# First tokens' softmax weights transposed in pairs of heads, and a fourth attention unit with float32 v

## The chip, the cores and the metric

The kernel runs on one core of a Trainium2 chip. The metric is the device time of one execution in microseconds. Before the change three executions took 577.93, 580.09 and 583.28 us, so the time before is their median, 580.09 us. One further execution was taken with the hardware profiler; it lasted 578.71 us, of which 576.9 us lie between the first and the last instruction that the profile shows.

## What is computed

Attention over 4 batches, 8 heads, 576 tokens of 64 elements, blended with a memory read, then a feed-forward block over all 2304 tokens:

```python
scores = scale * np.matmul(q, k.transpose(0, 1, 3, 2))      # causal
a = np.exp(scores - scores.max(-1, keepdims=True))
a /= a.sum(-1, keepdims=True) + 1e-09
local = np.matmul(a, v)
q_p = phi(q)
mem_out = einsum(q_p, M_prev) / (einsum(q_p, z_prev) + 1e-06)
g = 1.0 / (1.0 + np.exp(-beta))
attn = g * mem_out + (1 - g) * local
r = np.maximum(attn @ w_in, 0.0)                            # w_in 512x2048
out = (r * r) @ w_out                                       # w_out 2048x512
```

## The kernel before

The tokens of a batch are cut into tiles: the first 64 tokens (tile 0) and four tiles of 128 (tiles 1 to 4). The first 64 tokens of all four batches are done together, at the start, by `first_tokens` (L244); the rest is done by `attention` (L354), called once per unit. A unit is one batch, one pair of heads and either the tiles 1 and 2 ("lo"), 3 and 4 ("hi") or all four. The list `order` (L820) begins with the four lo units of batch 0 (units 0 to 3, here u0 to u3), then its four hi units (u4 to u7), and so on. The feed-forward block works on 256 tokens at a time: `moe(0)` on the first tokens, `moe(1)` on tiles 1 and 2 of batch 0, and so on, and at the end `moe_pair` on two blocks together. `moe(0)` is interleaved with the units u1 to u3 while the weights are still being loaded and split into a rounded and a rest part (`split_weight`, L169: ScalarE, VectorE and GpSimd work on each piece). `moe(1)` needs the output of u0 to u3, which goes to DRAM (`xd`) and is read back (`xn`), apart from the last pair of heads, u3, whose tile `memx` is transposed straight from SBUF (`prefetch`, L625, argument `tail`).

Each engine executes its instructions in a fixed order. That order is made when the program is built, by a scheduler that estimates when each instruction can run; it is not written out by hand, so an edit in one place can move instructions in others.

`first_tokens` packs two batches into a group g (two groups), with eight slots i (batch and pair of heads), and in each slot head 0 in the partitions 0 to 63 and head 1 in the partitions 64 to 127. `scores` (L272) fills `sp0`, `softmax` (L297) makes the weights `e` from it on VectorE and ScalarE, `outputs` (L311) transposes them by sixteen 64x64 matmuls with the identity (L315) into `px`, copies that on ScalarE to `wx` (L316), and accumulates M*f (L320) and v*wx (L321) in `xp`; from there ScalarE and VectorE make `xh` and `xl` (L326, L327), the input of `moe(0)`.

In `attention`, three flags go by the unit's place i in `order` (L837): `early` (i < 12), `sfull` (i < NES = 6: scores in float32) and `full` (i < NEF = 3, lo units alone: the softmax weights meet v in float32). With `full`, each tile's weights `e` are transposed on TensorE (L535, 64- and 128-column blocks, into `px`, named pxa), copied by ScalarE to `aT` (L540, named aF in the rows), and multiplied with `vv` in float32 (L579, acc). Without `full`, v is scaled to a power of two and split into two float16 halves `vs` (L405 to L428: vx, vt, vy, vz, vs), the weights are split into two float16 halves `a` (L558 on ScalarE, L560 on VectorE), a DMA transposes them (L564, `aT`), and L585 to L590 multiply on TensorE in float16; `s3` (L592) adds two column halves. Both ways end in L600, which adds to `memx`. The PSUM tiles pxa, pm (the memory read, L445), vt and acc all take turns in the two buffers of tag "av", so each waits until the one two places before it has been read. `kd` (the keys) has one buffer (KB = 1): the next unit's keys are loaded when the last scores of this unit are done.

## Time and profile before

| what | before |
|---|---|
| median of 3 executions | 580.09 us |
| profiled execution | 578.71 us, span 576.9 us |
| TensorE matmul (PE) busy | 550.8 us (95%) |
| VectorE (DVE) busy | 414.0 us (72%) |
| ScalarE (ACT) busy | 349.6 us (61%) |
| GpSimd (POOL) busy | 63.7 us (11%) |
| DMA, share of 16 engines' time | 49.7% |

Busy time is an average over stretches with different limits. In the profile's 40 slices of 14.4 us VectorE and ScalarE are near full in the first six, and TensorE is near full from the third to the last. A wait that the profile reports for an engine is idle time and what ended it; a matmul's end is modelled, so the distance between starts tells TensorE's pace better than the durations do. A float32 matmul shows as two instructions, a float32 transpose as one.

### The profile page before, as it was taken

What the parts mean: (1) busy time and instruction counts of PE and PEld (TensorE: products, weight loads), DVE (VectorE), ACT (ScalarE), POOL (GpSimd) and SP (SyncE); (2) the same over time, 40 slices, a digit from 0 to 9 for tenths busy, and PEclk for the clock granted to TensorE, in tenths of its full rate; (3) what the DMA queues carried; (4) which work ended last, traced back from release to release, by engine and by line L of the source; (5) the groups of instructions that cost most, each with busy time, mean ns of one, the idle gap of its engine ahead of it and who ended that gap; (6) DMA issues with size and microseconds to landing.
All of it is one profiled execution on the core that took longest, in us unless ns stands there. A gap on an engine that the chain in (4) does not pass through costs nothing.

```text
span 576.9 us, 11597 instructions
## 1 busy us (share of the span) xinstructions
PE 550.8 (95%) x4259; PEld 478.6 (83%) x4259; DVE 414.0 (72%) x1323; ACT 349.6 (61%) x792; POOL 63.7 (11%) x45
## 2 busy tenths in 40 slices
PE   5489998898999999999999999999999999999997
PEld 5378886787888888898988988889889898888885
DVE  6989989897989888989695988969787523212121
ACT  4589976767868767877567675665756222212213
POOL 3749560012010000000000000000000000000000
PEclk9999999799999999999999999999999999999999
DMA  8857654875665466676456736675244610000001
GB/s 310 341 192 286 228 168 111 174 162 136 138 150 159 109 183 151 149 185 168 110 108 124 149 78 163 115 189 143 56 84 83 128 37 1 36 2 0 1 0 73
DMA packets 124856, 74.71 MB, mean 129 GB/s; under 512 B 97152, under 2 KB 110464, under 8 KB 124800
## 3 DMA queue, kind: packets, MB, share of 16 engines
q1 hardware_dynamic: 124800, 73.98, 49.7%
q8 instruction: 33, 0.54, 0.4%
q14 instruction: 23, 0.19, 0.1%
HBM read 41.59 MB, written 8.78 MB: 87 GB/s over the span
## 4 chain that ended last, share of the span: by engine, by line
PE 63%; DVE 12%; ACT 10%; DMA 9%; issue 3%; POOL 1%; SPq 1%; ACTq 0%; DVEq 0%; POOLq 0%
PE oacc L677 8%; PE up L747 6%; PE up L749 6%; PE up L748 6%; PE oacc L737 6%; PE oacc L739 6%; PE oacc L738 6%; PE sp L479 5%; DMA vv<-in_qv_dram 4%; ACT e L520 3%; PE up L692 3%; PE up L691 3%; PE up L693 3%; PE acc L590 2%; PE pm L445 2%
## 5 line engine op out<-in xcount | busy, mean ns | idle before, releaser
L747 PE MATMUL up<-xh,w 128*128 128x256 f32 x448 | 129.5, 289 | 0.0
L748 PE MATMUL up<-xl,w 128*128 128x256 f32 x448 | 128.9, 288 | 0.0
L749 PE MATMUL up<-xh,w 128*128 128x256 f32 x448 | 128.4, 287 | 0.0
L520 ACT ACTIVATE e<-e,mx 128x320 f32<-128x320 f32 (+3 forms) x128 | 77.6, 608 | 50.1 <-DVE memx L600 34.1
L737 PE MATMUL oacc<-w,gh 128*128 128x512 f32 x224 | 89.9, 402 | 0.0
L747 PEld LDWEIGHTS up<-xh,w 128*128 128x128 f32 x448 | 86.0, 192 | 2.9 <-issue 0.6
L738 PE MATMUL oacc<-w,gh 128*128 128x512 f32 x224 | 88.4, 395 | 0.0
L748 PEld LDWEIGHTS up<-xl,w 128*128 128x128 f32 x448 | 86.1, 192 | 2.2
L739 PE MATMUL oacc<-w,gl 128*128 128x512 f32 x224 | 86.4, 397 | 0.4 <-DVE gl L759 0.4
L749 PEld LDWEIGHTS up<-xh,w 128*128 128x128 f32 x448 | 86.1, 192 | 0.7
L560 DVE SCALAR_TENSOR_TENSOR a<-e,a 128x128 f16<-128x128 f32 x116 | 64.1, 566 | 31.1 <-ACT a L558 30.1
L558 ACT ACTIVATE a<-e 128x128 f16<-128x128 f32 x116 | 55.0, 524 | 10.9 <-DMA aT<-a 9.9
L753 ACT ACTIVATE r<-up 128x512 f32<-128x512 f32 x56 | 32.7, 584 | 43.2 <-PE up L749 29.0
L702 DVE CAST gh<-r 128x512 fp32r<-128x512 f32 x15 | 6.4, 427 | 62.4 <-ACT r L701 62.4
L739 PEld LDWEIGHTS oacc<-w,gl 128*128 128x128 f32 x224 | 41.5, 188 | 9.0 <-DVE gl L759 0.9
L738 PEld LDWEIGHTS oacc<-w,gh 128*128 128x128 f32 x224 | 42.3, 189 | 6.6
L500 DVE CUSTOM_DVE_ANT_0 e<-sp,mask 128x320 f32<-128x320 f32 (+3 forms) x128 | 47.0, 417 | 0.9 <-PE sp L479 0.7
L737 PEld LDWEIGHTS oacc<-w,gh 128*128 128x128 f32 x224 | 42.3, 189 | 6.4
L700 ACT ACTIVATE r<-up 128x512 f32<-128x512 f32 x16 | 9.6, 597 | 60.8 <-PE up L693 60.8
L759 DVE TENSOR_TENSOR gl<-r,gh 128x512 fp32r<-128x512 f32 x56 | 38.9, 695 | 2.6 <-ACT gh L756 1.8
L677 PE MATMUL oacc<-w,gh 128*128 128x512 f32 x120 | 36.8, 389 | 0.0
L590 PE MATMUL acc<-vs,aT 128*128 128x128 f16 x302 | 36.7, 220 | 0.0
(153 smaller groups left out, 1160.2 us busy)
## 6 DMA issues: line engine op xcount, KB each, us to landing
raw<-in_w_in_dram SPq DMA_DIRECT2D x11, 512.0 KB, 7.2
vv<-in_qv_dram SPq DMA_DIRECT2D x16, 320.0 KB, 3.3
raw<-in_w_out_dram SPq DMA_DIRECT2D x9, 512.0 KB, 6.6
kd<-in_kk_dram SPq DMA_DIRECT2D x16, 288.0 KB, 3.1
out_dram<-o SPq DMA_DIRECT2D x16, 256.0 KB, 2.1
xd<-memx SPq DMA_DIRECT2D x31, 128.0 KB, 1.9
xn<-xd SPq DMA_DIRECT2D x14, 256.0 KB, 2.9
qm<-in_qv_dram SPq DMA_DIRECT2D x8, 321.0 KB, 2.9
```

The source lines that it names most:

```text
L500: nc.vector.tensor_tensor_reduce(out=e[:, h, ka:kb], in0=sps[:, h, cs], in1=mask[:, 448 - q0 + ka : 448 - q0 + kb], scale=-0.125, scalar=3 ...
L520: ex = nc.scalar.activation(e[:n, h, :ke], e[:n, h, :ke], AF.Exp, bias=bs, scale=-1.0, accum_out=sm[:n, h : h + 1])
L558: nc.scalar.mul(av[:, :, o0 : o0 + w], x, SC)
L560: nc.vector.scalar_tensor_tensor(out=av[:, :, o0 + w : o0 + 2 * w], in0=x, scalar=SC, in1=av[:, :, o0 : o0 + w], op0=ALU.mult, op1=ALU.sub ...
L590: nc.tensor.matmul(o2, aT[:, h * nb + c, :n], vs[:, h, c], start=False, stop=c == i)
L677: mms.append(nc.tensor.matmul(acc[t], g[:, ts], w_out_op(f, part), start=s0, stop=s1))
L737: nc.tensor.matmul(acc[t], gh[:, u, ts], w_out_op(f, 0), start=f == 0, stop=False)
L738: nc.tensor.matmul(acc[t], gh[:, u, ts], w_out_op(f, 1), start=False, stop=False)
L739: nc.tensor.matmul(acc[t], gl[:, u, ts], w_out_op(f, 0), start=False, stop=f == NF - 1)
L747: nc.tensor.matmul(up[:, u, :], w_in_op(f, k, 0), xh[:, k, :], start=k == 0, stop=False)
L748: nc.tensor.matmul(up[:, u, :], w_in_op(f, k, 0), xl[:, k, :], start=False, stop=False)
L749: nc.tensor.matmul(up[:, u, :], w_in_op(f, k, 1), xh[:, k, :], start=False, stop=k == NK - 1)
```

## The change

It does two things, and what they need. First, in `first_tokens` the scores are laid out so that a pair of slots shares a column block: slot i's two heads stand side by side, in the partition half that i's parity chooses. `outputs` can then transpose two heads of two slots at once: four 128x128 transposes (L316 of the changed kernel) instead of sixteen 64x64 matmuls for each group. `softmax` starts with two operations on 128x4x64 instead of one on 128x512, `v` is multiplied with half-column slices of `ex`, and the gate g1b gets its own columns in the beta table (12 columns become 20). Second, NEF goes from 3 to 4, so that u3 takes the `full` way as u0 to u2 do.

```diff
-NEF = 3
+NEF = 4
...
         def scores(g):
-            sp[g] = sp0[:, g]
+            sp[g] = sp0[:, :, g]
             q, k = part(g, 0), part(g, GD)
-            for i, hd in pairs():
-                nc.tensor.matmul(sp[g][hd, i], q[hd, i], k[hd, i], start=True, stop=True)
+            for i in range(0, GN, 2):
+                for u, h in ((0, 0), (1, 1), (1, 0), (0, 1)):
+                    hd, ud = (slice(x * D, (x + 1) * D) for x in (h, u))
+                    nc.tensor.matmul(sp0[ud, h, g, i // 2], q[hd, i + u], k[hd, i + u], start=True, stop=True)
...
-            nc.vector.scalar_tensor_tensor(
-                out=e, in0=sp[g], scalar=0.125, in1=mask0[:, None, :].to_broadcast(bc), op0=ALU.mult, op1=ALU.add
-            )
+            bc = [P, GN, D]
+            for h in range(2):
+                nc.vector.scalar_tensor_tensor(
+                    out=e.rearrange("p (j h) k -> p j h k", h=2)[:, :, h], in0=sp[g][:, h], scalar=0.125,
+                    in1=mask0[:, None, :].to_broadcast([P, GN // 2, D]), op0=ALU.mult, op1=ALU.add,
+                )
...
         def outputs(g):
-            ex = tp.tile([P, GN, D], F32, tag="wx", name="wx", bufs=2)
-            px = ps.tile([P, GN, D], F32, tag="up", name="px0", bufs=2)
-            for i, hd in pairs():
-                nc.tensor.matmul(px[hd, i], et[g][hd, i], ident[hd, hd], start=True, stop=True)
+            ex = tp.tile([P, GN // 2, P], F32, tag="wx", name="wx", bufs=2)
+            px = ps.tile([P, GN // 2, P], F32, tag="up", name="px0", bufs=2)
+            for j in range(GN // 2):
+                nc.tensor.transpose(px[:, j], et[g][:, 2 * j : 2 * j + 2].rearrange("p h k -> p (h k)"), ident)
             gate["s"] = nc.scalar.copy(ex, px)
...
-                gate["t"] = nc.tensor.matmul(xp[hd, i], v[hd, i], ex[hd, i], start=False, stop=True)
+                qs = slice(i % 2 * D, (i % 2 + 1) * D)
+                gate["t"] = nc.tensor.matmul(xp[hd, i], v[hd, i], ex[hd, i // 2, qs], start=False, stop=True)
```

The scheduler orders the program anew. Three places matter here (line numbers of the changed kernel differ by up to 3 from those before).

On ScalarE, in the first tokens: the copies wx of the two groups stand between the casts of the weights w_102 to w_105. Before:

```order
L187 CAST w_104<-raw_511 128x512
L187 CAST w_103<-raw_496 128x512
L316 COPY wx<-px_279 128x512
L187 CAST w_105<-raw_518 128x512
L316 COPY wx<-px_343 128x512
```

And in the changed kernel:

```order
L184 CAST w_104<-raw_488 128x512
L317 COPY wx<-px_279 128x512
L184 CAST w_103<-raw_473 128x512
L317 COPY wx<-px_332 128x512
L184 CAST w_105<-raw_495 128x512
```

Both copies stand one place earlier. On VectorE, beside it, the second group's scaling of w now stands behind the weight operation that it stood in front of, so w_104's cast can start one operation earlier; and on TensorE the first matmul of the second group that waits for f no longer stands ahead of the first group's matmuls with wx.

On TensorE, where `moe(0)` has run its last matmuls whose weights are there, and u3's products with v stand (oacc is `moe(0)`, sp are u4's second scores). Before:

```order
L739 MATMUL oacc<-w_1240,gl 128x512
L445 MATMUL pm<-qm,pe 128x130 x2
L585 LDWEIGHTS aT
L585 MATMUL acc<-vs,aT 128x128
...
L479 MATMUL sp<-kd,qm 128x512 x2
L585 LDWEIGHTS aT
...
L414 MATMUL vt<-identb,vx 128x128
L635 MATMUL px<-identr,xn 128x128 x6
L637 MATMUL px<-identr,memx 128x128
L445 MATMUL pm<-qm,pe 128x130 x2
L479 MATMUL sp<-kd,qm 128x448 x2
L479 MATMUL sp<-kd,qm 128x64 x2
L747 MATMUL up<-xh,w_1091 128x256
```

And in the changed kernel:

```order
L741 MATMUL oacc<-w_1203,gl 128x512
L537 MATMUL pxa<-identr,e 64x128
L537 MATMUL pxa<-identr,e 128x128 x2
L537 MATMUL pxa<-identr,e 64x128
L537 MATMUL pxa<-identr,e 128x128 x2
L581 MATMUL acc<-vv,aF 128x64 x6
...
L637 MATMUL px<-identr,xn 128x128 x6
L639 MATMUL px<-identr,memx 128x128
L481 MATMUL sp<-kd,qm 128x512 x2
L581 MATMUL acc<-vv,aF 128x64 x4
L416 LDWEIGHTS vx
L416 MATMUL vt<-identb,vx 128x128
L749 MATMUL up<-xh,w_1054 128x256
```

u3's sixteen float16 products have become ten float32 transposes and ten float32 products; u4's pm and u5's first scores, which stood ahead of the next 24 up matmuls of `moe(0)`, stand behind them, and u3's pm stands eight oacc matmuls earlier.

On ScalarE, the copies aF of u3 (64- and 128-partition forms) and what stands between them, in the changed kernel; before, u3 had no such copies, and its L558 stood further ahead:

```order
L390 ACTIVATE pe<-qm 128x256
L542 COPY aF<-pxa 64x128 x2
L542 COPY aF<-pxa 128x256 x2
L522 ACTIVATE e,sm<-e,mx 128x448 x2
L560 ACTIVATE a<-e 128x2x64
L560 ACTIVATE a<-e 128x2x384
L542 COPY aF<-pxa 64x128 x2
L542 COPY aF<-pxa 128x128 x2
L642 CAST xh<-px 128x4x128
```

The copies of u3's second tile stand behind the exponentials and the scaling of u4's first tile (448 and 384 columns).

## Rows read from the trace of the kernel before

**Rows 1.** The page, its first part: busy time of the engines.
```profile
PE 550.8 (95%) x4259; PEld 478.6 (83%) x4259; DVE 414.0 (72%) x1323; ACT 349.6 (61%) x792; POOL 63.7 (11%) x45
```

**Rows 2.** Who TensorE waited for, 95 to 104.5 us: total, times, longest (us).
```profile
PE pm L445 <- DVE s L592: 1.2, 1, 1.2
PE acc L585 <- DVE vs L427: 1.1, 1, 1.1
PE sp L479 <- DMA kd<-in_kk_dram: 1.0, 1, 1.0
PE px L635 <- DMA xn<-xd: 0.3, 1, 0.3
```

**Rows 3.** Windows: length, busy PE, PEld, DVE, ACT, POOL; granted clock, DMA share, GB/s.
```profile
102.30:108.90 6.60, 5.58 (x24) 4.43 (x24) 5.71 (x23) 4.59 (x10) 0.84 (x1) 0.50 0.69 155
108.90:115.40 6.50, 6.46 (x67) 5.29 (x66) 5.25 (x17) 5.72 (x13) 0.00 (x0) 0.99 0.93 158
```

**Rows 4.** Timeline, first tokens: start, length (us), engine, line, [idle before <- by].
```profile
12.54 1.28 DVE L300 SCALAR_TENSOR_TENSOR w<-sp,mask 128x512 f32<-128x512 f32 x2
...
15.92 0.61 DVE L182 TENSOR_SCALAR raw<-raw 128x512 uint32<-128x512 uint32 x1 [0.32 <-DMA raw<-in_w_in_dram]
...
25.22 2.94 PE L315 MATMUL px<-identr,w 64*64 64x64 f32 x64 [0.35 <-DVE w L309]
...
26.41 0.66 ACT L187 CAST w<-raw 128x512 fp32r<-128x512 f32 x1 [1.87 <-DVE raw L184]
...
28.63 0.58 ACT L316 COPY wx<-px 128x512 f32<-128x512 f32 x1
...
29.26 0.27 PE L321 MATMUL xp<-wx,tr 64*64 64x64 f32 x1 [0.25 <-ACT wx L316]
```

**Rows 5.** Windows for line L315 alone: length, busy PE, PEld; granted clock, DMA share, GB/s.
```profile
25.20:26.20 1.00, 0.98 (x18) 0.98 (x20) 1.00 0.92 375
...
27.20:28.00 0.80, 0.80 (x32) 0.80 (x30) 1.00 0.05 20
```

**Rows 6.** Timeline of TensorE: what follows the last matmul of xp.
```profile
33.15 1.13 PE L479 MATMUL sp<-kd,qm 64*128 64x320 f32 x8
```

**Rows 7.** Timeline of TensorE, u3's float16 products and what follows each stretch.
```profile
96.97 0.22 PE L585 MATMUL acc<-vs,aT 128*128 128x128 f16 x1 [1.11 <-DVE vs L427]
...
97.72 1.13 PE L479 MATMUL sp<-kd,qm 64*128 64x512 f32 x4
98.78 0.23 PE L585 MATMUL acc<-vs,aT 128*128 128x128 f16 x1
...
99.07 0.22 PE L414 MATMUL vt<-identb,vx 128*128 128x128 bf16 x1
```

**Rows 8.** Timeline of TensorE, float32 products of u0 and what follows each stretch.
```profile
45.06 1.38 PE L579 MATMUL acc<-vv,aF 64*128 64x64 f32 x8
46.37 0.50 PE L739 MATMUL oacc<-w,gl 128*128 128x512 f32 x1
...
47.40 0.56 PE L579 MATMUL acc<-vv,aF 128*128 128x64 f32 x4
47.79 0.38 PE L535 MATMUL pxa<-identr,e 128*64 128x128 f32 x2
...
52.22 1.52 PE L579 MATMUL acc<-vv,aF 64*128 64x64 f32 x8
53.58 0.67 PE L445 MATMUL pm<-qm,pe 128*128 128x130 f32 x4
```

**Rows 9.** Timeline of TensorE and ScalarE: transposes and copies of u2; one scaling L558.
```profile
84.83 0.60 PE L535 MATMUL pxa<-identr,e 128*64 128x128 f32 x4
85.18 0.36 PE L747 MATMUL up<-xh,w 128*128 128x256 f32 x1
...
88.06 0.72 ACT L540 COPY aF<-pxa 64x128 f32<-64x128 f32 x4
...
98.14 1.04 ACT L558 ACTIVATE a<-e 128x128 f16<-128x128 f32 x2 [2.27 <-DMA aT<-a]
```

## The prediction

> **What bounds the kernel now.** I read the page's busy times first: TensorE's matmuls are busy 550.8 of 576.9 us, 95% [rows 1]. No other engine comes near, so the kernel ends when TensorE's work ends, and a change can move the time in three ways: it changes TensorE's work, its idle time, or the clock that it is granted. Next I read the table of waits over the stretch in which u3 meets v, since half of the change is there. It names 3.6 us in four waits (1.2 + 1.1 + 1.0 + 0.3) between 95 and 104.5 us [rows 2]. [...] Last I read the timeline of the first tokens, where TensorE waits for others. Its matmuls with the weights, L315, start at 25.22; ScalarE's copy wx(0) starts at 28.63 and takes 0.58; the first product with wx stands at 29.26 and waited for that copy [rows 4]; the last one ends at 33.15, where the scores of the next unit begin [rows 6].

> The profiled execution took 578.71 us. That is 1.4 below the median of the three runs (580.09); the sums below start from 578.71, and the range allows for that distance.

> **Part A, the first tokens.** Sixteen matmuls for a group become four transposes. Before, wx(0) stands behind the casts of w_104 and w_103 on ScalarE; the first of them starts at 26.41 and waited for VectorE [rows 4]. Now wx(0) stands behind w_104's cast alone, and on VectorE that cast's input stands one operation further ahead; a pass over 512 columns takes 0.61 there [rows 4], so the cast starts near 25.8, ends near 26.5 (0.66), and wx(0) ends near 27.0 instead of 29.21: 2.2 us earlier. wx(1) takes about the place that wx(0) had, ending at 29.2. The first product with wx no longer has the second group's wait for f ahead of it. From 29.26 to 33.15 [rows 4, 6] the 64 matmuls of both groups take 3.89, or 1.95 for a group. At the same pace the first group now runs 27.05 to 29.0, the second 29.2 to 31.15: **2.0 us earlier**. That is the best end.

> The worst end comes from the pace. Within L315 there are 18 matmuls in 1.0 us from 25.2, and 32 in 0.8 us from 27.2 [rows 5]: it doubles during L315, though the granted clock column reads 1.00 in both windows. I take that to be the rise of TensorE's clock to its higher level, after rb and 40 matmuls of L315. After the change only eight transposes stand where 64 matmul records stood (one for each transpose, two for each matmul), so there is less work ahead of xp, and the rise can fall into xp itself. If all of xp ran at the slow pace, it would take 7.8 us from 27.05, to 34.85: 1.7 later than before. If the rise comes at the end of the first group, that group ends at 30.95 and the second at 32.9: 0.25 earlier; if in its middle, 1.0 to 1.5 earlier. I take **-0.5** (bounds -2.0 and +1.7), since work like that of 25.2 to 27.0 had brought the rise before. What stands behind xp (ScalarE's and VectorE's xh and xl, the first up matmuls, and SP's load of the keys behind the scores) is released by it, and moves along.

> [...]

> VectorE gets two passes of 256 columns for each pass of 512 in the softmax (1.28 us for the two passes of before [rows 4]). Two halves cost at least the same and at most twice that, +0 to +1.3; I take +0.1, which the idle 0.32 us ahead of 15.92, ended by a DMA, hides [rows 4]. Without that cover it would move L315's start, and so A, by the same. The gate's beta table is one operation less; nothing.

> **Part B, u3 with v in float32.** TensorE's work:
> - taken away: the float16 products, 0.75 (96.97 to 97.72) and 0.29 (98.78 to 99.07) [rows 7], and vt, about 0.2: -1.24;
> - added: ten transposes; four take 0.35 in u2 (84.83 to 85.18) [rows 9], so 0.9;
> - added: ten products; in u0 tile 2's took 1.31 (45.06 to 46.37) and 0.39 (47.40 to 47.79), tile 1's 1.36 (52.22 to 53.58) [rows 8]: 3.06. Together +3.96 - 1.24 = **+2.7**.

> TensorE's waits: for vs, for s and for the keys' DMA [rows 2]. vs and s are steps of the float16 way and don't exist any more for u3. The keys' load is released by the last scores of the unit, which move up with them; xn comes from DRAM after u2, and is 0.3 us late only because nothing stands ahead of it. So **-3.6** at most, and the stretch is filled with 4 us of matmuls where it was thin. Does the clock then fall to 0.50? The fill brings me to say no: **-2.8** (bounds -2.8 and 0).

> New waits. The products follow their transposes at once, so TensorE waits for ScalarE's copies aF: for the first tile two of 64x128 (four took 0.72 in u2 [rows 9], so 0.36) and two of 128x256 (half of a 128x512 copy's 0.58 [rows 4] each): 0.9. For the second tile ScalarE first has u4's two exponentials and the scaling L558, 1.04 for two of 128 columns [rows 9], while TensorE has only six matmuls of px and the scores to do; I take 0.8 more. Together **+1.7** (bounds 0.9, the first tile alone, and 3.6, as much as TensorE waits there now). VectorE loses vx, vt, vs, L560 and L592 of u3, ScalarE exchanges L558 for the copies, two DMA transposes go: all beside TensorE.

> B: -3.6 - 2.8 + 2.7 + 1.7 = **-2.0**.

> **Part C, given back.** u4 uses float16 as before, and TensorE comes to it earlier than VectorE does; the wait for vs that u3 had (1.1 [rows 2]) can come back there: 0 to +1.1; I take **+0.5**.

> Sum: 578.71 - 0.5 - 2.0 + 0.5 = 576.7, say **576.7 us**, 0.6% below the median.

> **Rivals.**
> - R1, the clock stays low through all of xp, +1.7 in place of -0.5: 578.9. For it: only eight transposes are left ahead of xp [rows 5]. Against: rb's matmuls, too, stand before them, and xp's own matmuls bring a rise as L315's did. 14%.
> - R2, everything works: xp at full pace (-2.0), new waits only 0.9 (B -2.8), nothing given back: 573.9. For it: each of these steps has its row, and TensorE at 95% [rows 1] passes on whatever it saves. 25%.
> - R3, on the other side: ScalarE's queue holds u3's second copies back behind u4's exponentials, the stretch stays thin, TensorE waits 3.6 as before and the clock falls as before. Then B is the added work, +2.7, and the time 578.71 - 0.5 + 2.7 + 0.5 = 581.4. It decides from the point at which new waits exceed 3.7 with the clock kept, or 0.9 with the clock lost; of 1.7 expected, that is not far. 15%.
> - R4, the gain is given back later: VectorE and ScalarE are 72% and 61% busy as a mean [rows 1], and both are near full in the first 80 us. If u4 to u7 wait for them, TensorE arrives early and waits, B and C cancel: 578.2. 14%.

> **How the numbers follow.** My forecast has 32%, the four rivals 68%. Best case of all bounds: -2.0 (A), -3.7 (B with no new wait at all), 0 (C): 573.0. Worst: +1.7, +2.7, +1.1: 584.2. The range must leave out no more than 2 in 10: from 571.5 (the best case, and 1.4 of the distance between one execution and a median) to 582.5 (R3 with the whole of C). All but R3 lie below the profiled execution or within 0.2 of it. What a measurement of this kernel can tell from no change is about 1%: faster is below 574.3, slower above 585.9. Faster then holds most of R2 and a little of the forecast: 0.24. Slower lies 1.7 beyond even the worst sum; the distance between one execution and a median reaches most of that way: 0.08. Within 1%: 0.68.

> **What would show it.** wx(0)'s end (27.0 against 29.21) and the spacing of xp's matmuls show A: if the whole of xp takes 3.9 us, R1 is wrong; if the first scores behind it begin at 33.15 or later, A is. In the stretch 93 to 106, the table of waits must lose vs and s and show aF copies on ScalarE at 1.7; a granted clock near 1.00 where 0.50 stood shows B's clock term. If the clock still falls, I am 2.8 too low; if it falls somewhere else, in the units behind, too. For C, the wait of L585 for vs grows in u4. The forecast is wrong as a whole if the new order moves stalls to places that no part here names.

## The result, and the profile after

The changed kernel takes 587.27 us (median of 4 runs, 586.07 to 587.82) against 580.36 us before: ratio 1.0117, 95% interval 1.0086 to 1.0147. It is slower, by 1.2%; 576.7 had been forecast, and the range ended at 582.5.

The page of the changed kernel, first busy times and then the granted clock in 40 slices:

```profile
span 585.2 us, 11501 instructions
PE 556.0 (95%) x4216; PEld 483.0 (83%) x4216; DVE 408.3 (70%) x1310; ACT 350.7 (60%) x795; POOL 62.2 (11%) x45
...
PEclk9999998798999999999999999999999999999999
```

VectorE lost 5.7 us of work, as foreseen, and TensorE gained 5.2 [rows 1]. Windows around the float32 products of u3 and behind them (columns as in [rows 3]):

```profile
99.20:109.50 10.30, 9.80 (x41) 8.08 (x40) 6.40 (x19) 5.50 (x14) 0.84 (x1) 0.50 0.45 107
109.50:116.00 6.50, 6.50 (x51) 4.61 (x50) 6.22 (x24) 4.83 (x11) 0.00 (x0) 1.00 0.72 141
136.70:140.30 3.60, 3.60 (x20) 3.21 (x19) 3.57 (x14) 2.23 (x4) 0.00 (x0) 0.53 0.31 72
```

The granted clock falls all the same, for longer than in [rows 3], and a second time at 136.7. TensorE's waits, 90 to 106 us (answering to [rows 2]) and then 106 to 236 us, first of the changed kernel, last of the kernel before:

```profile
PE acc L581 <- ACT aF L542: 0.6, 1, 0.6
PE px L637 <- DMA xn<-xd: 0.5, 1, 0.5
```

```profile
PE sp L481 <- DVE vx L414: 1.7, 1, 1.7
PE oacc L741 <- DVE gl L761: 1.7, 1, 1.7
PE acc L587 <- DVE s L594: 1.5, 1, 1.5
PE vt L416 <- DVE vx L414: 0.6, 1, 0.6
PE sp L481 <- DVE ql L374: 0.5, 1, 0.5
PE acc L587 <- DVE vs L429: 0.3, 1, 0.3
```

```profile
PE acc L585 <- DVE memx L456: 1.0, 2, 0.7
PE sp L479 <- DVE mx L500: 0.7, 1, 0.7
PE oacc L739 <- DVE gl L759: 0.4, 1, 0.4
PE sp L479 <- DVE ql L372: 0.3, 1, 0.3
```

At u3 the waits went from 3.6 to 1.1 us, but from 106 to 236 they went from 2.4 to 6.3. Summed over all of TensorE's records in the two traces (low clock: half the time of the matmuls that run at 0.50; work: what is left). The half is an estimate from the 0.50, and a little high for the up matmuls, which in the kernel before begin 0.21 us apart at 0.50 (107.2 to 108.7 us) and 0.12 at 1.00 (109.6 to 110.3):

| | before | after | difference |
|---|---|---|---|
| first up matmul of `moe(0)` | 34.2 | 34.0 | -0.2 |
| waits behind it | 7.8 | 9.4 | +1.6 |
| lost to the low clock | 2.8 | 6.4 | +3.6 |
| work at full clock | 528.1 | 531.0 | +2.9 |
| last matmul begins | 573.0 | 580.9 | +7.9 |

Each column is one execution: the one before is 1.65 us below its median (580.36), the changed one 0.3 below (587.27), so part of the 7.9 is the choice of executions. By this table the clock is the main loss. The experiments show that the loss does not need it: waits and low clock are for the most part exchanged for each other, and something else makes their sum grow.

The chain that ended last, by engine, of the kernel before and of the changed one, says why an exchange is possible:

```profile
PE 63%; DVE 12%; ACT 10%; DMA 9%; issue 3%; POOL 1%; SPq 1%; ACTq 0%; DVEq 0%; POOLq 0%
```

```profile
PE 51%; DVE 22%; DMA 13%; ACT 9%; issue 3%; SPq 1%; POOL 1%; ACTq 0%; DVEq 0%
```

TensorE is busy 95% of the time in both, yet the chain leaves it for half or a third of the span, for VectorE, ScalarE and DMAs: in the attention units they pace it.

### The profile page after: what moved, and what is told of

Same layout as the page of the kernel before. It is cut to its first block, busy times and chain, and to the rows that moved or that the text cites. A ratio compares the mean times of both kernels' runs of the same rounds, so it can differ in the third digit from the quotient of the medians.

```text
span 585.2 us, 11501 instructions
## 1 busy us (share of the span) xinstructions
PE 556.0 (95%) x4216; PEld 483.0 (83%) x4216; DVE 408.3 (70%) x1310; ACT 350.7 (60%) x795; POOL 62.2 (11%) x45
## 4 chain that ended last, share of the span: by engine, by line
PE 51%; DVE 22%; DMA 13%; ACT 9%; issue 3%; SPq 1%; POOL 1%; ACTq 0%; DVEq 0%
PE oacc L679 7%; DMA aT<-a 5%; DMA vv<-in_qv_dram 4%; PE up L749 4%; PE oacc L741 4%; PE up L751 4%; PE oacc L740 4%; PE up L750 4%; PE oacc L739 4%; DVE a L562 4%; DVE e L502 4%; PE sp L481 3%; ACT a L560 3%; PE up L695 2%; PE up L693 2%
## 5 line engine op out<-in xcount | busy, mean ns | idle before, releaser
L562 DVE SCALAR_TENSOR_TENSOR a<-e,a 128x128 f16<-128x128 f32 x112 | 62.9, 573 | 32.4 <-ACT a L560 31.5
L560 ACT ACTIVATE a<-e 128x128 f16<-128x128 f32 x112 | 53.5, 528 | 11.3 <-DMA aT<-a 10.8
L592 PE MATMUL acc<-vs,aT 128*128 128x128 f16 x296 | 35.7, 220 | 0.0
```

Source lines behind the costliest of these rows:

```text
L560: nc.scalar.mul(av[:, :, o0 : o0 + w], x, SC)
L562: nc.vector.scalar_tensor_tensor(out=av[:, :, o0 + w : o0 + 2 * w], in0=x, scalar=SC, in1=av[:, :, o0 : o0 + w], op0=ALU.mult, op1=ALU.sub ...
```

## The experiments

Each kernel ran on the chip beside the kernel before; ratios are to it, with 95% intervals. "Order" is the order of instructions on the five engines; where it is called the same, it is the same instruction by instruction.

### One part alone, and the clock

```diff
e1: -NEF = 4   +NEF = 3        (changed kernel)
e2: -NEF = 3   +NEF = 4        (kernel before)
e3: -    nc.tensor.transpose(px[:cw, x, :n], e[:n, h, c0 : c0 + cw], ident)     (u3 alone)
    +    nc.tensor.matmul(px[:cw, x, :n], e[:n, h, c0 : c0 + cw], ident, start=True, stop=True)
e4: the same exchange for the eight transposes px of the first tokens
```

> The changed kernel with NEF = 3: only the first tokens' paired transposes are left of the change. Theory: the 7 us come from u3's float32 way, so this kernel is at 580.2, within 1 us of the kernel before; its xp runs at the low clock in its first half and ends 0.2 us before that of before. Rival: the pairing costs the time, through the order of the rest that the scheduler makes anew; then it is at 585 or above.

> The kernel before with NEF = 4: only u3's float32 way. Theory: it carries the whole loss, 587.5, with a stretch of granted clock 0.50 of some 10 us from about 99 us on. Rival: with the first tokens as before the stretch lies 0.2 us otherwise and the clock doesn't fall longer than before; then 582 or less.

Measured: the pairs alone 1.0069 (1.0045 to 1.0093), the fourth unit alone 0.9991 (0.9961 to 1.0021). I had it the wrong way round. u3's float32 way costs nothing that shows, and the paired transposes, with the longer table that they need, cost 0.7%.

> The changed kernel, with u3's ten transposes alone done as ordinary float32 matmuls with the identity instead of the transpose mode; the order on TensorE is the same. [...]

Measured: 1.0108 (1.0079 to 1.0137). The order is that of the changed kernel but for thirteen places on VectorE ahead of 112 us. Windows of e3, then of the changed kernel, 95 to 110 us:

```profile
95.00:110.00 15.00, 13.71 (x92) 10.51 (x91) 10.39 (x34) 10.81 (x27) 0.87 (x2) 1.00 0.50 133
```

```profile
95.00:110.00 15.00, 13.88 (x69) 11.30 (x69) 9.79 (x31) 8.62 (x24) 0.84 (x1) 0.66 0.48 123
```

The granted clock is 1.00 over this window of e3, against 0.66, and the time does not come back: waits behind the first up matmul grow from 9.4 to 15.1 us while the loss to the low clock falls from 6.4 to 1.7 (e3's trace is of the slowest of its four executions). So the time is lost without the fall of the clock too. What made the clock fall in the changed kernel is not shown: e5 below, with the changed kernel's instructions in the same order everywhere, had 1.00 from 99.2 to 109.5 us too.

That does not make the clock free. Over the 289 executions of the experiments and of the kernel before beside them, and within one kernel and round, a mean granted clock lower by 0.01 goes with 1.4 us more (interval 1.0 to 1.8), where 0.01 of 580 us would be 5.8 if nothing were given back. But it does not tell the two kernels apart: the mean is 0.992 over 126 executions of the kernel before and 0.9925 over the four of the changed one.

> The changed kernel, with the first tokens' eight paired transposes done as ordinary float32 matmuls with the identity. [...]

Measured: 1.0156 (1.0115 to 1.0197); the first up matmul at 34.95 instead of 34.04. The order changed as well, so this kernel doesn't show what the exchange alone does to TensorE's pace or to the time.

### The addresses

The beta table grows from 12 to 20 columns of 4 bytes. With those 32 bytes more, every SBUF tile behind the table lies 32 bytes further. In the kernel before, a (at 40448 and 45056), the larger aT (49664), e, vv, vs and the weights lie on multiples of 256 bytes; in the changed kernel none does. e1 has the shift and e2 has not.

```diff
e5: -    gpm = cp.tile([P, NP + H + GN], F32, name="gpm")                    (changed kernel)
    +    gpm = cp.tile([P, NP + H + GN + 8], F32, name="gpm")[:, : NP + H + GN]
e6: the same 8 unused columns in the kernel before;   e7: in e1 (pairs alone)
e8: 56 unused columns in the changed kernel;   e9: 24;   e12: 56 in e1;   e16: 8 in e2
e10: -    kh, kl = (at.tile([P, S], F32R, tag=t, name=t) for t in ("kh", "kl"))   (kernel before)
     +    kh, kl = (at.tile([P, S + 8], F32R, tag=t, name=t)[:, :S] for t in ("kh", "kl"))
```

> The changed kernel with eight unused columns more in the beta table (28 columns of 4 bytes instead of 20), so that every SBUF tile behind it lies 32 bytes further, on a multiple of 64 bytes again as before the change; same instructions in the same order on all engines. Theory of the addresses: the beta table's growth from 12 to 20 columns moved a, aT, e, the weights and all else to 32 bytes behind a multiple of 64, and that makes the DMA transposes aT dearer (3.82 us before, 4.08 after); here they are at 3.8 again and the time is 576 to 580, below or at that of before. Rival, the order: the scheduler's new order costs the time; then this runs like the changed kernel, 587.

> The kernel before with eight unused columns in the beta table (20 instead of 12), so that every tile behind it lies 32 bytes further, as in the changed kernel; same instructions in the same order on all engines. Theory of the addresses: aT's transposes go from 3.82 to 4.1 us, and the time from 581 to 584 to 588 without any other change. Rival, the order: nothing changes, 581.

> The paired transposes alone (NEF = 3), with the beta table at 28 columns, so that the tiles lie on multiples of 64 bytes again. Theory of the addresses: the loss of the paired transposes alone (585.2 against 581.4) goes; the time is 579 to 581.5. Rival, the order: 585 as without the eight columns.

Measured: e6 1.0084 (1.0051 to 1.0116): the kernel before, moved by 32 bytes and otherwise the same, loses 5 us. But e5 stays at 1.0108 (1.0076 to 1.0139) and e7 at 1.0073 (1.0045 to 1.0101): 64 bytes from the old place is no better than 32. So the address matters, and multiples of 64 bytes are not enough. TensorE's waits in e6 that the kernel before has not, or shorter (106 to 236 us, then one at 405 us):

```profile
PE acc L585 <- DVE memx L456: 1.7, 2, 1.4
PE acc L585 <- DMA aT<-a: 1.1, 1, 1.1
```

```profile
405.19 0.22 PE L585 MATMUL acc<-vs,aT 128*128 128x128 f16 x1 [1.05 <-DVE memx L456]
```

Matmul by matmul, e6's trace is 1.8 us behind at 230 us and 5.3 at 500; most of the second part comes between 351 and 405 us, where the kernel before does not wait. The DMA part of the page of the kernel before, then of e6 (share of 16 engines' time; us from issue to landing):

```profile
q1 hardware_dynamic: 124800, 73.98, 49.7%
...
aT<-a SPq DMA_TRANSPOSE x58, 3.9
```

```profile
q1 hardware_dynamic: 124800, 73.98, 51.2%
...
aT<-a SPq DMA_TRANSPOSE x58, 4.1
```

The same packets and bytes take longer, and among the frequent DMAs the transposes do so most: issued by SP in 1.73 us as a mean before and 1.95 in e6, landing after 3.8 and 4.2, and 48 of the 58 take longer than the same one before. The loads of vv and kd, whose tiles moved as well, take 3.5 and 3.4 us in both. In SP's queue the next DMA starts behind them, and so later too: in the kernel before two transposes take SP 3.69 us from 205.97 on, and the store of xd starts at 209.99, 4.02 us after the first; in e6 they take 4.42 from 207.59 on, and the store starts at 212.06, 4.47 after.

> The changed kernel with 56 unused columns more in the beta table (76 instead of 20): every tile behind it lies 256 bytes from its place in the kernel before. Same instructions in the same order on all engines as the changed kernel. [...] Before, a, the larger aT, e, vv and the weights lie on multiples of 256; shifts of 32 and 64 take that away. Theory of 256 bytes: here aT's transposes are back at 1.75 us of issue and 3.8 us to landing, and the time is 577 to 581. Rival, the order: 587 as the changed kernel.

> The same with 24 unused columns (44 in all): every tile behind the beta table lies 128 bytes from its place in the kernel before. Theory of 256 bytes: as slow as the changed kernel, 586 to 588, with 1.9 us of issue for aT. Rival, that 128 bytes are enough: 577 to 581.

> The kernel before with eight unused columns at the end of kh and of kl: the tiles behind them (xh, xl, xn, gh, gl, the weights) lie 64 bytes further; a, aT, e, vv and vs stay where they are. Same instructions, same order. Theory of the transposes: only a and aT matter, so nothing changes, 581 and 1.73 us of issue for aT. Rival, that the weights or xn matter: 584 to 587.

Measured: e8 1.0054 (1.0025 to 1.0083), half way between its two expectations; e9 1.0096 (1.0063 to 1.0130), e10 1.0014 (0.9988 to 1.0041). e9, then e8:

```profile
q1 hardware_dynamic: 122688, 73.46, 49.4%
...
aT<-a SPq DMA_TRANSPOSE x56, 4.2
```

```profile
q1 hardware_dynamic: 122688, 73.46, 47.6%
...
aT<-a SPq DMA_TRANSPOSE x56, 3.8
```

By the transposes 128 bytes are not enough and 256 are (the intervals of the two times overlap); and the weights, xh, xl and xn may move without a cost that shows. So of the shifts tried, only 256 bytes brings the transposes back, 3.8 us against 4.2 at 128 with the same packets, and a, aT or another tile ahead of the weights is what counts. That it is a and aT is argued, not isolated by a run; the transposes are where the trace shows it. "On the grid" stands below for a and the larger aT on multiples of 256 bytes, "off" for anything else.

Across all runs the split has no exception. The transposes take, as means from issue to landing, all of them and then those during which no packet of the instruction queue 8 falls (why that matters comes below):

| kernels | a and the larger aT | all, us | without such a packet, us |
|---|---|---|---|
| before, e2, e8, e10 to e15, e17, e22 | on the grid | 3.7 to 3.8 | 3.4 to 3.6 |
| after, e1, e3 to e7, e9, e16 | 32, 64 or 128 bytes off | 4.1 to 4.2 | 3.8 to 3.9 |

> The kernel before with NEF = 4 and 20 columns in the beta table (8 unused), tiles 32 bytes further; order as with NEF = 4 alone. Theory of the addresses: 4 to 5 us above NEF = 4 alone (579.8), so 583.5 to 585.5, with 1.9 us of issue for aT. Rival, that the address costs only where the order is tight (u3 in float16): 580 to 581.

Measured: 1.0080 (1.0054 to 1.0105), against 0.9991 for e2, which differs in the addresses alone. So the 32 bytes cost 0.84% in the kernel before, 0.9% in e2, and e8 gives back 0.6% of the changed kernel's 1.2%.

```diff
e11: changed kernel,  e13: kernel e2,  e14: kernel before; in each, with unused columns in gpm:
-    qm = at.tile([P, 2 * ZW + SQ], F32, tag="qm", name="qm", bufs=QB)
+    qm = at.tile([P, 704], F32, tag="qm", name="qm", bufs=QB)[:, : 2 * ZW + SQ]
-    vx = at.tile([P, 1], F32, tag="vx", name="vx", bufs=2)
+    vx = at.tile([P, 16], F32, tag="vx", name="vx", bufs=2)[:, :1]
-    nm = at.tile([P, 3, 2], F32, tag="nm", name="nm", bufs=2)
+    nm = at.tile([P, 16, 2], F32, tag="nm", name="nm", bufs=2)[:, :3]
```

> The changed kernel with unused columns in the beta table, qm, vx and nm so that a, both aT, memx, kd, qm, vv, vs and e all start on multiples of 256 bytes (before, memx, kd, qm and the smaller aT did not). Same instructions, same order. Theory of 256 bytes: as e8 or better by up to 3 us (575 to 580), with aT's issue at or below 1.75 us. Rival: as the changed kernel, 587.

> The kernel before with NEF = 4, and unused columns so that a, both aT, memx, kd, qm, vv, vs and e all start on multiples of 256 bytes. Theory of 256 bytes: at or below NEF = 4 alone, 577 to 580, the fastest of all. Rival: the smaller aT, kd, qm and memx don't matter, 579.8.

> The kernel before with unused columns so that a, both aT, memx, kd, qm, vv, vs and e all start on multiples of 256 bytes; same instructions, same order. If the tiles that before did not lie there (the smaller aT, memx, kd, qm) matter, 577 to 579; if a and the larger aT are all that matters, 580 to 581.5.

Measured: e11 1.0047 (1.0015 to 1.0078), e13 0.9984 (0.9964 to 1.0004), e14 1.0004 (0.9982 to 1.0025). Beside e8, e2 and the kernel before they gain nothing that can be told: the smaller aT, memx, kd and qm don't matter. e13 is the fastest kernel tried by its ratio, 579.94 us, though not surely faster than before.

### What the pairs still cost on the grid

> The paired transposes alone (NEF = 3) with 76 columns in the beta table: tiles 256 bytes from their places before. Same instructions and order as the pairs alone. If the pairs' loss (1.0069) is the addresses' alone, this is at 580 to 581.5 (ratio 0.997 to 1.002). If the remade order costs as well, as the changed kernel's 1.0054 at plus 256 suggests, it stays at 583 to 585.

Measured: 1.0059 (1.0033 to 1.0084). With its addresses mended the pairs alone still lose 0.6%, as e8 does. They lost 0.7% off the grid (e1), so here the grid is worth 0.1% by the ratios, with overlapping intervals, although the transposes got shorter (4.08 to 3.78 us as a mean). How much of the transposes' time becomes the kernel's time thus seems to depend on the order. Splitting one VectorE operation in two makes the scheduler write the program in another order, in e15 nearly all of it, in e17 (beside e2) the first 112 us; two kernels have that order without the pairs:

```diff
e15 (kernel before) and e17 (kernel e2):
-            nc.vector.scalar_tensor_tensor(
-                out=e, in0=sp[g], scalar=0.125, in1=mask0[:, None, :].to_broadcast(bc), op0=ALU.mult, op1=ALU.add
-            )
+            for i in range(0, GN, GN // 2):
+                nc.vector.scalar_tensor_tensor(
+                    out=e[:, i : i + GN // 2], in0=sp[g][:, i : i + GN // 2], scalar=0.125,
+                    in1=mask0[:, None, :].to_broadcast([P, GN // 2, D]), op0=ALU.mult, op1=ALU.add,
+                )
```

> The kernel before with one edit: the first softmax operation on VectorE in two halves of 256 columns instead of one of 512. Its addresses are those of before, its matmuls too, but the scheduler then makes the same order behind the first tokens as with the paired transposes. Theory that the remade order costs: 583 to 585 here, without any transpose, wait or address changed. Rival, that the pairing itself (its clock, its copies) costs: 581 to 581.7.

> The kernel before with NEF = 4 and the first softmax operation in two halves of 256 columns: addresses of before, first tokens' matmuls of before, and behind the first tokens the order that the changed kernel has. If the order carries what is left of the changed kernel's loss at plus 256 (1.0054), this is at 1.003 to 1.006, 582 to 583.5. If the pairing itself carries it, it is at NEF = 4 alone, 0.998 to 1.001, 579 to 580.5.

Measured: e15 1.0027 (1.0006 to 1.0047), e17 1.0015 (0.9995 to 1.0035). These two and e12 lie between their two expectations. By the ratios the order carries some 0.2 to 0.3%, and 0.3 to 0.4% are left for the pairs themselves, but neither share is clear of the noise: e12 and e15, run in the same round, have medians of 582.47 and 582.32, and e17's interval holds 1. e17 and e8 differ by nothing but the first tokens and a shift of 256 bytes. In their traces e8 has the lead there: its first up matmul starts at 32.87, e17's at 34.58. Of that lead 1.3 us are left at 80 us and 0.6 at 85, behind ScalarE's wait for weights at 66 us; in e17 the first of these two rows of e8 waits 0.2 us and the second nothing. At 88 us the lead is gone; e8's clock is at 0.50 from 86.8 to 90.2:

```profile
66.25 0.69 ACT L180 ACTIVATE raw<-raw 128x512 f32<-128x512 f32 x1 [1.16 <-DMA raw<-in_w_in_dram]
```

```profile
84.11 0.50 PE L739 MATMUL oacc<-w,gh 128*128 128x512 f32 x1 [0.49 <-ACT gh L758]
```

And e8 waits near 220 us where e17 does not: it is 0.7 us ahead of e17 at 220 and 2.3 behind at 230. TensorE's waits from 200 to 236 us, e8 and then e17:

```profile
PE acc L587 <- DVE s L594: 1.4, 1, 1.4
PE sp L481 <- DVE ql L374: 0.5, 1, 0.5
```

```profile
PE sp L481 <- DVE ql L374: 0.4, 1, 0.4
```

Behind these waits e8's clock falls as well. The same window of e8 and then of e17 (columns as in [rows 3]):

```profile
223.30:226.70 3.40, 3.40 (x30) 3.34 (x27) 3.40 (x12) 1.41 (x5) 0.00 (x0) 0.50 0.30 68
```

```profile
223.30:226.70 3.40, 3.40 (x26) 3.06 (x24) 3.40 (x16) 1.76 (x5) 0.00 (x0) 1.00 0.70 160
```

At 0.50 for 3.4 us the loss is up to 1.7 us, an estimate (half of 3.4). TensorE's only waits from 200 to 236 us are the 1.4 and 0.5 us above, so I see nothing there that gives it back: here the low clock does seem to cost time.

The DMA view of 207 to 216 us (busy tenths and GB/s in 40 slices), e8 and then e17:

```profile
DMA  0000000001999999999999800000699999920000
GB/s 0 0 0 0 0 0 0 0 0 36 272 291 289 289 287 288 284 280 254 202 304 192 2 0 0 8 9 10 146 291 289 291 291 310 350 50 0 0 0 0
...
q8 instruction: 1, 0.02, 0.7%
...
aT<-a SPq DMA_TRANSPOSE x2, 5.4
```

```profile
DMA  0000000000008999999999999999999000000594
GB/s 0 0 0 0 0 0 0 0 0 0 0 1 209 291 290 290 291 288 288 286 272 272 278 167 290 291 287 281 277 305 271 18 0 0 0 0 0 118 155 127
...
aT<-a SPq DMA_TRANSPOSE x2, 3.9
```

In e8 the two transposes stop for over 1 us in their middle (2, 0, 0, 8, 9, 10 GB/s), and an instruction packet lies there: in this part of the run queue 8 fetches every 13 to 19 us, 16 KB at a time. That it is TensorE's program is my estimate: the 33 packets come to 64 bytes for each of some 8,400 matmul and weight load records. The paired transposes take 56 matmuls and as many weight loads out of TensorE's program, and the fetches fall elsewhere: at 211.7 us in e8, at 205.7 in e17, ahead of the transposes. The changed kernel, e1, e5, e7 and e9 have such a fetch in the same pair, and its first transpose takes 6.3 or 6.4 us there; e6, off the grid without a fetch, has 4.8. The kernel before has one elsewhere, at 108.7 us, in a transpose of 5.7.

```diff
e22: changed kernel with 56 unused columns in gpm (e8), and
+        for t in range(2):
+            wt = ps.tile([P, NK, P], F32, tag="up", name="wt", bufs=2)
+            for j in range(28):
+                nc.tensor.matmul(wt[:, 0, j : j + 1], identb, identb[:, j : j + 1], start=True, stop=True)
         sp0 = ps.tile([P, 2, ng, GN // 2, D], F32, tag="s", name="sp0")
```

> The changed kernel at plus 256 bytes, with 56 tiny bfloat16 matmuls (one column, into an unused tile) at the very start of TensorE's work: its instruction count is back at that of NEF = 4 alone (4272 matmul records and as many weight loads). Order behind the first tokens nearly as there. In the trace of the changed kernel at plus 256 an instruction fetch at 211.7 us falls into two transposes of aT, which take 5.7 and 5.1 us instead of 4.0 and 3.7, and TensorE then waits 1.4 and 0.5 us for s. Theory of the fetch: it now falls near 206, ahead of the transposes, these take 4 us, and the time is 580.5 to 582. Rival, that this fetch costs nothing in the end: 584 as before.

Measured: 1.0026 (1.0007 to 1.0046), 582.63 us. Its DMA view of 209 to 218 us:

```profile
DMA  0000000000399999999999999999940000006957
...
aT<-a SPq DMA_TRANSPOSE x2, 3.9
```

The fetch is at 207.9, the hole, TensorE's wait for s and the fall of the clock behind it are gone, and by the ratios half of what e8 lost to before is back, though 56 matmuls were added; the time is slower than expected by 0.6 us. The intervals of e8 and e22 overlap, and the order of e22 also differs from e8's in the first 112 us. So the traces show what the fetch does to these transposes, and its share of the time is likely but not measured.

## Why the prediction was wrong, point by point

- **What bounds the kernel.** "The kernel ends when TensorE's work ends" was the step behind all terms, and it fails up to about 226 us, where the last larger wait of the changed kernel is (in e6 again up to 405). There TensorE at 95% is paced by the units on VectorE, ScalarE and DMA; what it gains in one place it waits for in the next (at u3 3.6 us of waits became 1.1, behind it 2.4 became 6.3). R4 named this and got 14%.
- **The step priced at nothing.** "The gate's beta table is one operation less; nothing" is the one that failed most. Its eight new columns moved a, the larger aT and others behind the table off multiples of 256 bytes: 0.6% of the time in the changed kernel (e8), 0.8 to 0.9% in two others (e6, e16), hardly any in the pairs alone (e12). No part and no rival had the addresses. The new order had no price either, though the prediction's last sign names it: stalls at places that no part names.
- **Part A.** Forecast -0.5; the first scores behind xp start at 32.97 instead of 33.15 [rows 6], -0.2. The steps were right: wx(0) was copied from 26.47 to 27.06 (27.0 was forecast), and the first half of xp ran at half the pace of the second. Windows for L323, products with wx, in the changed kernel:

```profile
27.70:30.90 3.20, 3.20 (x31) 3.20 (x32) 1.00 0.03 8
31.00:32.90 1.90, 1.90 (x35) 1.90 (x33) 1.00 0.00 0
```

 31 instructions in 3.2 us and then 35 in 1.9: the pace doubles at 31 us, at the end of the first group, and as in [rows 5] the granted clock column does not show it. The trace's own record of the clock begins at that moment, at 30.97 us (at 27.15 in the kernel before), and the column reads 1.00 ahead of it; that the pace is the clock's is thus my reading, not a figure of the trace. R1 was wrong. The size differs by execution: with the same instructions the first scores start at 31.80 in e8 and at 33.51 in e9. No size of the term shows in the time: e8's lead of 1.7 us is gone at 88 us.
- **Part B.** The work was sized well (+2.7 forecast, +2.9 left over in the table for the whole program). The waits at u3 fell to 1.1, better than the 1.7 forecast. The clock term failed: -2.8 was forecast, half of the 5.58 us at 0.50 in [rows 3]. No run shows this term; by the table the low clock cost 3.6 more, as the clock fell at 99.2 us in spite of a TensorE that was busy (9.80 of 10.30 us), and where it kept 1.00 (e3, e5) the time was 1.0108 all the same. TensorE's rows ahead of that fall:

```profile
95.03 0.82 PE L537 MATMUL pxa<-identr,e 128*64 128x128 f32 x6
96.47 1.97 PE L581 MATMUL acc<-vv,aF 64*128 64x64 f32 x12 [0.63 <-ACT aF L542]
98.28 0.60 PE L537 MATMUL pxa<-identr,e 128*64 128x128 f32 x4
98.87 0.45 PE L637 MATMUL px<-identr,xn 128*128 128x128 f32 x3
99.81 0.49 PE L637 MATMUL px<-identr,xn 128*128 128x128 f32 x2 [0.49 <-DMA xn<-xd]
```

 Transposes, products of 64 columns, transposes, and 1.1 us of waits. Which of these let it fall stays open: the same instructions kept 1.00 in e5. The loss does not hang on it, as e3 and e5 show; the whole of part B, alone, is worth between -0.4% and +0.2% (e2), and -0.35% was forecast.
- **Part C.** +0.5 was forecast for one wait in u4. The waits from 106 to 236 us grew by 3.9, of which the one named, for vs, is 0.3.
- **R3** had the sign and the fall of the clock, but not the cause: ScalarE's copies held TensorE up by 0.6 us, and the waits at u3 fell to 1.1 instead of staying at 3.6.

By the ratios, what the changed kernel loses is so made up: the addresses 0.6%, the remade order 0.2 to 0.3%, what the pairs do beside that 0.3 to 0.4%, u3 in float32 -0.1%. The first is shown; that something is left on the grid is shown too (e8, e11, e12), but how it divides between order and pairs, and what of it is the instruction fetch near 210 us, stays open, as each part has an interval of 0.3 to 0.4% to either side.

## What to carry to other kernels

A change of a tile's size can move all addresses behind it (here 32 bytes, 0.84% of the time in e6): write down where the tiles of DMAs lie before and after, and before believing any other reason run the old kernel with nothing but its tiles moved. Where the chain leaves the busiest engine for a third of the span, price a gain on that engine at zero until the stretch's own pace is found. And where a scheduler orders the program, a harmless edit that makes the same new order is the control that tells the order from the idea.
